# Ten stores at the end of a long convolution and state-space kernel: issued by SyncE instead of GpSimd

## The chip, the cores and the metric

The kernel runs on one core of a Trainium2 chip. The core has five engines, each with its own instruction stream: TensorE (PE in the profile: matmuls; PEld: loading of their stationary operand), VectorE (DVE), ScalarE (ACT), GpSimd (POOL) and SyncE (SP). They meet through semaphores. Data moves between HBM and the on-chip memory by DMA transfers: here SyncE or GpSimd issues them, and 16 DMA engines carry them. The profile counts SyncE's transfers under "hardware_dynamic" (queue q1) and GpSimd's under "software_dynamic" (q0). The metric is the device time of one execution, in microseconds.

## The reference, cut to what matters

Two independent heads work on sequences of 2048 steps and 1024 channels, and their outputs stand side by side in one array of 2048 rows and 2048 columns, in bf16.

```python
# head A: short shift convolution of k, times v; long convolution by FFT; gate with q
kv = k_shift * v
y  = irfft(rfft(pad(kv)) * rfft(pad(ssm_k)))[:S] + kv * ssm_D
a  = q * y
# head B: diagonal complex recurrence
Bu = einsum("bld,pd->blp", x, B_bar)
h[t] = Lam_bar * h[t-1] + Bu[t]
b  = 2 * real(einsum("blp,dp->bld", h, Cmat)) + x * Dskip
out = concatenate([a, b], axis=-1)
```

## The kernel before, in words

Head A turns the long convolution into two levels of small discrete Fourier transforms, done as matmuls against constant tables. Between the levels the data goes through scratch arrays in HBM (`Ys_kv`, `Ys_h`, `Vs`), which is how it is rearranged. The last level is the part that matters here: for each of 16 row groups `n2` SyncE loads a tile from `Vs` (task `vl`, line 694), TensorE multiplies it with a constant (`a3`, line 706) in two halves of 512 columns, ScalarE copies each half out of a PSUM bank (`a3e`, line 713), and for each pair `r` of row groups VectorE multiplies with q in place (`qm`, line 715). The result of a pair, 128 partitions by 2 rows of 1024 columns, 512 KB, is stored by GpSimd into head A's half of the output (`ost`, line 716). There are eight such stores.

Head B goes through the sequence in 16 chunks of 128 steps. For chunk `i`, TensorE projects the input, VectorE rotates, scans and rotates back (`r1` to `r4`, `sc`), TensorE forms the output in two halves of 512 columns, each in four parts (`y`, lines 518 and 521), and ScalarE copies each half out of its PSUM bank into one arena unit (`ye`, line 527). GpSimd stores the whole chunk, 128 rows of 1024 columns, 256 KB, into head B's half of the output (`yst`, line 529). There are sixteen of these.

All tiles lie in one arena of 53 units of 2 KB per partition. The order of the work is written out by hand in one long string, `ORDER`: a word is a task with its arguments and, after a colon, the arena units (a), PSUM banks (p) and other slots that it takes. Tasks are put on their engines in that order, and the framework adds the semaphore waits that the data needs. Each engine carries out its own instructions in order. DMA transfers of SyncE and of GpSimd each use eight semaphores in turn, so a transfer also waits until the one eight before it on the same engine has landed. At the end of the program (line 777) SyncE waits for all transfers, each engine drains, and a handshake led by GpSimd closes the execution.

At the very end, SyncE's last load is `vl.0`. Behind it in `ORDER` come eight stores of head A and the stores of chunks 14 and 15, all on GpSimd:

```python
E["yst"] = lambda i: gpd(out_b[i * T:(i + 1) * T, :], st.pop(("yo", i)))
E["ysp"] = lambda i: spd(out_b[i * T:(i + 1) * T, :], st.pop(("yo", i)))
E["ost"] = lambda r: gpd(oar[:, 2 * r:2 * r + 2, :], st["ot", r])
E["osp"] = lambda r: spd(oar[:, 2 * r:2 * r + 2, :], st["ot", r])
```

Here `gpd` is a transfer issued by GpSimd and `spd` one issued by SyncE; `ysp` and `osp` are there in the kernel before, but `ORDER` doesn't use them.

Of the kernel before, what the change touches and what calls it, by code (L numbers as in the profile page):

```python
# [158 lines left out]
y.14.0.0:p0 y.14.0.1 r2.15:h0 cy.15 vl.7:a40 a3.7.0:p7 y.14.0.2 a3e.15.1 qm.5 ye.13.0 vl.5:a42 y.14.0.3 a3e.12.1 ye.14.0:a34 a3.5.0:p3 vl.13:a28  # L159
a3.13.1:p4 a3.7.1:p5 a3.13.0:p2 a3e.13.0 yst.11 vl.3:a30 a3.3.0:p1 a3.3.1:p6 a3.5.1:p0 a3e.3.0 a3e.7.0:a2 a3e.5.0 vl.6:a10 a3.6.0:p2 a3.6.1:p1 a3e.6.0  # L160
y.14.1.0:p7 a3e.6.1 vl.1:a8 a3e.3.1 y.14.1.1 sc.15.1 vl.9:a16 y.14.1.2 a3e.7.1 a3.9.1:p3 y.14.1.3 yst.13 a3.1.1:p2 a3.9.0:p1 a3.1.0:p6 sc.15.0 a3e.9.1
a3e.5.1 qm.7 vl.0:a48 a3.0.1:p5 a3.0.0:p3 a3e.0.1:a36 r3.15:a12 a3e.9.0 ost.7 r4.15 a3e.0.0 y.15.0.0:p0 y.15.0.1 y.15.0.2 y.15.1.0:p5 y.15.0.3
y.15.1.1 y.15.1.2 ost.5 qm.1 ost.1 qm.3 ye.14.1 ost.3 a3e.1.1 qm.2 a3e.1.0 ost.2 qm.4 qm.0 yst.14 ost.4 a3e.13.1 qm.6 ye.15.0:a52 ost.0 ost.6 y.15.1.3
ye.15.1 yst.15
"""


def full_kernel(ctx, tc, A_q, A_k, A_v, A_shift_k, A_ssm_k, A_ssm_D, B_x, B_Lre, B_Lim, B_Bre, B_Bim,
# [7 lines left out]
    T = 128  # L176
# [6 lines left out]
    out_b = out[0][:, D:2 * D]  # L183
    spd = nc.sync.dma_start
# [45 lines left out]
    st = {}  # L230
# [12 lines left out]
    E = {}  # L243
# [283 lines left out]
        return nc.scalar.copy(st["yo", i][:, dh * 512:(dh + 1) * 512], st.pop(("py", i, dh)))  # L527
    E["ye"] = ye
    E["yst"] = lambda i: gpd(out_b[i * T:(i + 1) * T, :], st.pop(("yo", i)))
    E["ysp"] = lambda i: spd(out_b[i * T:(i + 1) * T, :], st.pop(("yo", i)))  # L530

    def kp(r):
# [180 lines left out]
        return nc.scalar.copy(st["ot", r][:, n2 % 2, dh * 512:(dh + 1) * 512], st.pop(("po", n2, dh)))  # L713
    E["a3e"] = a3e
    E["qm"] = lambda r: nc.vector.tensor_mul(st["ot", r], st["ot", r], st["qt", r])
    E["ost"] = lambda r: gpd(oar[:, 2 * r:2 * r + 2, :], st["ot", r])
    E["osp"] = lambda r: spd(oar[:, 2 * r:2 * r + 2, :], st["ot", r])

# [10 lines left out]
@with_exitstack  # L729
def kernel(  # L730
    ctx: ExitStack,
    tc: tile.TileContext,
    A_q: bass.AP,
    A_k: bass.AP,
    A_v: bass.AP,
    A_shift_k: bass.AP,
    A_ssm_k: bass.AP,
    A_ssm_D: bass.AP,
    B_x: bass.AP,
    B_Lambda_re: bass.AP,  # L740
    B_Lambda_im: bass.AP,
    B_B_re: bass.AP,
    B_B_im: bass.AP,
    B_C_re: bass.AP,
    B_C_im: bass.AP,
    B_log_dt: bass.AP,
    B_Dskip: bass.AP,
    out: bass.AP,
):
    full_kernel(ctx, tc, A_q, A_k, A_v, A_shift_k, A_ssm_k, A_ssm_D, B_x, B_Lambda_re, B_Lambda_im,  # L750
                B_B_re, B_B_im, B_C_re, B_C_im, B_log_dt, B_Dskip, out)
# [30 lines left out]
```

## Time and profile before

| | |
|---|---|
| time, median of 3 runs | 359.53 us (358.28 to 361.29) |
| the profiled execution, its own time | 357.83 us |
| its span, first to last instruction | 356.1 us |
| granted TensorE clock, mean | 0.995 |
| TensorE busy | 333.2 us (94%) |
| VectorE, ScalarE, GpSimd busy | 314.1, 285.4, 87.5 us |
| moved by DMA | 104.10 MB, mean 292 GB/s |

Times of instructions are given in microseconds from the start of the span. A line of the timeline has start, duration, engine, source line, operation, tiles written and read, and in brackets how long the engine had been idle before and for whom it waited. A line with shapes and three numbers joined by slashes gives durations in ns as minimum, median and maximum, and then the first and last start. A stretch shows its length, then for PE, PEld, DVE, ACT and POOL the busy time and the number of instructions, and at the end the granted clock, the busy share of the DMA engines and GB/s. An engine name with a q (SPq, POOLq) is that engine's instruction queue: semaphore and DMA instructions that are not counted as busy.

### The profile page before, as it was taken

How to read it: one execution, taken by the hardware profiler on the slowest of the kernel's cores; microseconds unless marked ns; L12 is line 12 of the kernel's file. 1: busy time of each engine (PE TensorE's matmuls, PEld its weight loads, DVE VectorE, ACT ScalarE, POOL GpSimd, SP SyncE). 2: the span in 40 equal slices, each digit the busy share in tenths (PEclk: the TensorE clock that was granted, in tenths of full speed). 3: DMA queues.
4: the chain of work that ended last, by engine and by line, in shares of the span. 5: the costliest groups of instructions: out<-in, count | busy, mean ns of one | idle time of the engine just before them, and what ended most of it. 6: DMA issues, size and time to landing. Idle time of an engine off the chain costs nothing.

```text
span 356.1 us, 10361 instructions
## 1 busy us (share of the span) xinstructions
PE 333.2 (94%) x4378; PEld 232.8 (65%) x4393; DVE 314.1 (88%) x239; ACT 285.4 (80%) x547; POOL 87.5 (25%) x142
## 2 busy tenths in 40 slices
PE   5999999999999999999979999898989998999991
PEld 2889998465947669766835667464766875944440
DVE  4899999999999999999987997987498769997970
ACT  5899998257799989999578998888989996546550
POOL 5000000021515333436140205121421422300250
PEclk9999999999999999999999999999999999999997
DMA  6999987598999999999989999989889998899973
GB/s 212 319 262 299 234 135 202 195 298 190 297 224 353 317 326 296 276 299 322 323 278 337 327 328 352 307 298 324 312 321 308 349 345 290 330 317 389 371 284 148
DMA packets 62826, 104.10 MB, mean 292 GB/s; under 512 B 29582, under 2 KB 31646, under 8 KB 62780
## 3 DMA queue, kind: packets, MB, share of 16 engines
q1 hardware_dynamic: 50012, 59.78, 59.0%
q0 software_dynamic: 12768, 43.67, 33.6%
q8 instruction: 34, 0.56, 0.7%
q14 instruction: 12, 0.10, 0.1%
HBM read 53.62 MB, written 35.13 MB: 249 GB/s over the span
## 4 chain that ended last, share of the span: by engine, by line
PE 63%; DMA 13%; ACT 10%; issue 6%; DVE 4%; POOL 2%; SPq 1%; POOLq 0%; DVEq 0%; ACTq 0%
PE bank L444 24%; PE bank L518 13%; PE bank L499 6%; DMA wslot<-a_c_W 4%; DMA arena<-arena 4%; PE bank L573 4%; PE bank L611 4%; DMA arena<-Xs 3%; ACT BT L414 3%; PE bank L678 2%; PE bank L595 2%; PE bank L640 2%; DVE gslot L472 2%; PE bank L398 2%; DMA arena<-in_B_B_re_dram 2%
## 5 line engine op out<-in xcount | busy, mean ns | idle before, releaser
L444 PEld LDWEIGHTS <-BT 128*128 128x128 bf16 x2048 | 117.9, 98 | 11.2 <-issue 4.3
L444 PE MATMUL bank<-arena,BT 128*128 128x128 bf16 x2048 | 123.8, 220 | 1.5 <-ACT BT L414 0.8
L472 DVE TENSOR_TENSOR_SCAN gslot<-rtab,gslot 128x1040 bf16<-128x1040 f32 x32 | 72.7, 2310 | 3.9 <-ACT gslot L468 3.5
L518 PE MATMUL bank<-CT,gslot 128*128 128x512 bf16 x275 | 68.7, 379 | 0.7
L499 PE MATMUL bank<-CT,gslot 64*64 64x512 bf16 x896 | 56.3, 376 | 0.4 <-DVE gslot L478 0.4
L666 DVE TENSOR_TENSOR arena<-arena 128x4096 bf16<-128x4096 bf16 x16 | 36.6, 2290 | 17.4 <-ACT arena L656 7.6
L446 ACT CAST arena<-bank 128x512 bf16<-128x512 f32 x64 | 39.0, 641 | 10.1 <-PE bank L444 9.8
L518 PEld LDWEIGHTS <-gslot 128*128 128x128 bf16 x288 | 26.3, 98 | 27.4
L499 PEld LDWEIGHTS <-gslot 64*64 64x64 bf16 x896 | 28.6, 107 | 20.6 <-DVE gslot L478 0.9
L656 ACT CAST arena<-bank 128x512 bf16<-128x512 f32 x64 | 36.2, 658 | 5.6 <-PE bank L640 4.7
L649 ACT CAST arena<-bank 128x512 bf16<-128x512 f32 x64 | 35.0, 637 | 4.7 <-issue 1.5
L617 ACT CAST arena<-bank 128x512 bf16<-128x512 f32 x64 | 35.2, 672 | 4.1 <-PE bank L611 2.9
L686 ACT CAST arena<-bank 128x512 bf16<-128x512 f32 x64 | 35.5, 660 | 3.2 <-PE bank L678 3.0
L579 ACT CAST arena<-bank 128x512 bf16<-128x512 f32 x64 | 35.7, 629 | 2.9 <-PE bank L573 2.9
L459 DVE TENSOR_TENSOR arena<-gslot,Z 128x4096 bf16<-128x4096 bf16 x16 | 36.6, 2289 | 0.7
L459 DVE TENSOR_TENSOR arena<-arena,Z 128x4096 bf16<-128x4096 bf16 x16 | 36.5, 2282 | 0.7 <-ACT arena L446 0.6
L660 POOL DMA_DIRECT2D arena<-arena x32 | 17.4, 547 | 70.6 <-ACT arena L649 60.9
L620 POOL DMA_DIRECT2D Ys_h<-arena x32 | 23.3, 730 | 35.8 <-ACT arena L617 35.8
L640 PE MATMUL bank<-arena,wslot 64*64 64x512 bf16 x256 | 23.7, 382 | 6.8 <-DMA wslot<-a_c_W 4.1
L553 DVE TENSOR_TENSOR arena<-arena 128x4096 bf16<-128x4096 bf16 (+3 forms) x16 | 30.0, 1880 | 0.0
L527 ACT CAST arena<-bank 128x512 bf16<-128x512 f32 x32 | 19.8, 645 | 11.4 <-PE bank L521 9.9
L582 POOL DMA_DIRECT2D Ys_kv<-arena x16 | 11.1, 695 | 64.1 <-ACT arena L579 64.0
(101 smaller groups left out, 421.1 us busy)
## 6 DMA issues: line engine op xcount, KB each, us to landing
Ys_kv<-arena POOLq DMA_DIRECT2D x16, 512.0 KB, 6.5
Ys_h<-arena POOLq DMA_DIRECT2D x32, 256.0 KB, 4.7
arena<-Ys_h SPq DMA_DIRECT2D x16, 512.0 KB, 5.4
arena<-arena POOLq DMA_DIRECT2D x32, 256.0 KB, 4.6
arena<-Ys_kv SPq DMA_DIRECT2D x16, 512.0 KB, 7.7
Vs<-arena POOLq DMA_DIRECT2D x16, 512.0 KB, 6.5
arena<-Vs SPq DMA_DIRECT2D x16, 512.0 KB, 6.7
arena<-in_A_k_dram SPq DMA_DIRECT2D x8, 512.0 KB, 5.4
```

The lines of the kernel that those rows point to most:

```text
L444: nc.tensor.matmul(pu[:, w, jl, :], BT[:, 2 * jp + jl, w, d, :], xT[:, d, :], start=(d == 0), stop=(d == ND - 1))
L446: E["ue"] = lambda i, jp: nc.scalar.copy(st["u", i][:, :, 2 * jp:2 * jp + 2, :], st.pop(("pu", i, jp)))
L459: nc.vector.tensor_mul(m, s_, win(Z))
L472: nc.vector.tensor_tensor_scan(gf, rtab[:].rearrange("p j t -> p (j t)"), gf, 0.0, ALU.mult, ALU.add)
L499: mm = nc.tensor.matmul(st["py", i, dh][64 * c:64 * c + 64, :], h[rows, w, j, 2 + 64 * c:66 + 64 * c], CT[rows, j, w, dh * 512:(dh + 1) * ...
L518: nc.tensor.matmul(py, h[:, w, j, 2:GW], CT[:, j, w, dh * 512:(dh + 1) * 512], start=(j == 0 and w == 0), stop=False)
L579: return nc.scalar.copy(st["ysb", n2][:, p, dh * 512:(dh + 1) * 512], st.pop(("pa", n2, p, dh)))
L617: return nc.scalar.copy(st["yh", hf, s][:, p, e, :], st.pop(("pb", hf, s, e, p)))
L649: return nc.scalar.copy(st["hab", i][:, 0, a, l, :], st.pop(("ps", "h", g, l)))
L656: return nc.scalar.copy(st["x16", i][:, a, l, :], st.pop(("ps", "k", g, l)))
L666: nc.vector.tensor_mul(hab, st.pop(("x16", i)).rearrange("p a l d -> p (a l d)").unsqueeze(1).to_broadcast([P, 2, 2 * D]), hab)
L686: return nc.scalar.copy(st["vsb", i][:, a, dh * 512:(dh + 1) * 512], st.pop(("pv", g, dh)))
```

## The change

The ten stores behind SyncE's last load are issued by SyncE. Eight `ost` become `osp`, `yst.14` becomes `ysp.14`, and the store of the last chunk, `yst.15`, becomes two stores of 512 columns each, by a new task `yh`: the first half stands ahead of the last part of the matmuls of that chunk, the second half at the end. The order of all other tasks and the arena units are as before. GpSimd's last instruction before the end of the program is then `yst.13`.

```diff
@@ -159,9 +159,9 @@
-a3e.5.1 qm.7 vl.0:a48 a3.0.1:p5 a3.0.0:p3 a3e.0.1:a36 r3.15:a12 a3e.9.0 ost.7 r4.15 a3e.0.0 y.15.0.0:p0 y.15.0.1 y.15.0.2 y.15.1.0:p5 y.15.0.3
-y.15.1.1 y.15.1.2 ost.5 qm.1 ost.1 qm.3 ye.14.1 ost.3 a3e.1.1 qm.2 a3e.1.0 ost.2 qm.4 qm.0 yst.14 ost.4 a3e.13.1 qm.6 ye.15.0:a52 ost.0 ost.6 y.15.1.3
-ye.15.1 yst.15
+a3e.5.1 qm.7 vl.0:a48 a3.0.1:p5 a3.0.0:p3 a3e.0.1:a36 r3.15:a12 a3e.9.0 osp.7 r4.15 a3e.0.0 y.15.0.0:p0 y.15.0.1 y.15.0.2 y.15.1.0:p5 y.15.0.3
+y.15.1.1 y.15.1.2 osp.5 qm.1 osp.1 qm.3 ye.14.1 osp.3 a3e.1.1 qm.2 a3e.1.0 osp.2 qm.4 qm.0 ysp.14 osp.4 a3e.13.1 qm.6 ye.15.0:a52 osp.0 osp.6 yh.15.0
+y.15.1.3 ye.15.1 yh.15.1
@@ -527,6 +527,7 @@
     E["yst"] = lambda i: gpd(out_b[i * T:(i + 1) * T, :], st.pop(("yo", i)))
+    E["yh"] = lambda i, dh: spd(out_b[i * T:(i + 1) * T, dh * 512:(dh + 1) * 512], st["yo", i][:, dh * 512:(dh + 1) * 512])
     E["ysp"] = lambda i: spd(out_b[i * T:(i + 1) * T, :], st.pop(("yo", i)))
```

## The prediction

> **What bounds the kernel now.** I read the head of the page first, then the stretches at the end, then what each engine does behind its last useful instruction.
>
> ```profile
> span 356.1 us, 10361 instructions
> ...
> PE 333.2 (94%) x4378; PEld 232.8 (65%) x4393; DVE 314.1 (88%) x239; ACT 285.4 (80%) x547; POOL 87.5 (25%) x142
> ```
>
> ```profile
> 342.00:346.00 4.00, 3.95 (x23) 1.99 (x23) 3.26 (x3) 2.45 (x6) 1.90 (x4) 1.00 0.95 352
> 346.00:350.00 4.00, 2.64 (x15) 1.12 (x13) 0.32 (x1) 1.14 (x2) 1.37 (x3) 1.00 0.94 354
> ```
>
> TensorE bounds everything up to its own last matmul: it is busy for 3.95 of 4.00 us between 342 and 346, and for 2.64 us after 346, which is until 348.64. The column before the last says that the DMA engines are 94 to 95% busy there, with stores alone. No store stands before a matmul, so until 348.64 the stores are covered. What they decide is the 7.4 us between 348.64 and the end at 356.05. In order of time those begin so:
>
> ```profile
> 337.59 3.49 DVE L715 TENSOR_TENSOR arena<-arena 128x2048 bf16<-128x2048 bf16 x3
> ...
> 343.96 2.36 DVE L715 TENSOR_TENSOR arena<-arena 128x2048 bf16<-128x2048 bf16 x2 [0.74 <-ACT arena L713]
> ...
> 345.97 0.58 ACT L527 CAST arena<-bank 128x512 bf16<-128x512 f32 x1 [1.55 <-issue]
> ...
> 346.62 0.72 POOL L716 DMA_DIRECT2D out_dram<-arena  x1 [0.41 <-DVE arena L715]
> ...
> 348.42 0.22 PE L521 MATMUL bank<-Dd,arena 128*128 128x128 bf16 x1
> ...
> 348.68 0.58 ACT L527 CAST arena<-bank 128x512 bf16<-128x512 f32 x1 [2.13 <-PE bank L521]
> 349.56 0.57 POOL L529 DMA_DIRECT2D out_dram<-arena  x1 [2.22 <-ACT arena L527]
> ```
>
> The last matmul ends at 348.64, the last eviction at 349.26, and GpSimd takes up the last store 0.30 us later. The next two answers are for that store alone (from its issue to landing) and for line 777, the end of the program (ns as min/median/max, then first and last start):
>
> ```profile
> L529 POOL DMA_DIRECT2D out_dram<-arena x1: 570/570/570, 349.6 to 349.6; - x1
> ...
> DMA to landing us min/median/max: 2.3/2.3/2.3
> ```
>
> ```profile
> L777 SPq EVENT_SEMAPHORE  x6: 27/28/2082, 349.5 to 349.8; - x6
> ```
>
> ```profile
> L777 SPq DRAIN  x2: 7/10/13, 352.1 to 352.2; - x2
> L777 POOLq DRAIN  x1: 5730/5730/5730, 349.5 to 349.5; - x1
> ```
>
> ```profile
> L777 POOLq EVENT_SEMAPHORE  x4: 17/17/17, 355.3 to 355.9; - x4
> L777 POOLq DRAIN  x3: 51/99/5730, 349.5 to 355.8; - x3
> ```
>
> Here is the point of the whole case. The last store has landed at 349.56 + 2.3 = 351.9. SyncE, which collects all DMAs, sees it (the last of six checks, begun at 349.8, takes 2.08 us, until 351.9) and has drained at 352.2. Then nothing happens for three microseconds, until GpSimd's own drain ends: 349.54 + 5.73 = 355.27. Only then GpSimd takes the others' signals (355.3) and the closing handshake runs, 356.05 - 355.27 = 0.8 us. The wait view says the same from SyncE's side: 3.3 us at line 777. It names TensorE as the releaser, though TensorE had long been done, and the row above it is SyncE's wait for the stores:
>
> ```profile
> SPq L777 <- DMA out_dram<-arena: 23.4, 2, 21.3
> SPq L777 <- PEq L777: 3.7, 2, 3.3
> ```
>
> So the end now has two arms that close in order: the store at 352.2, GpSimd's drain at 355.27. GpSimd's other two drains took 51 and 99 ns with nothing issued since the one before; the long one stands right behind a store.
>
> **The change part by part.** *GpSimd.* Ten stores leave it: eight of 512 KB and two of 256 KB. Its last instruction is then the store of B tile 13, with these rows (issue in ns and its start, then to landing):
>
> ```profile
> L529 POOL DMA_DIRECT2D out_dram<-arena x1: 540/540/540, 329.8 to 329.8; - x1
> ...
> DMA to landing us min/median/max: 6.3/6.3/6.3
> ```
>
> It lands at 336.0. Before, the drain ended 355.27 - 351.9 = 3.4 us after the landing and 355.27 - 350.13 = 5.1 us behind the issue. By either measure it ends between 335 and 340 in the changed kernel, hidden under ten microseconds of TensorE. The arm worth 355.27 - 352.2 = 3.1 us is gone, and next late is SyncE's arm.
>
> *SyncE.* It gains eleven issues. The prices are those of its loads, its last load among them; the first row is the product that its first store waits for:
>
> ```profile
> 333.01 1.20 DVE L715 TENSOR_TENSOR arena<-arena 128x2048 bf16<-128x2048 bf16 x1
> ```
>
> ```profile
> L716 POOL DMA_DIRECT2D out_dram<-arena x8: 710/725/732, 334.5 to 346.6; - x8
> ```
>
> ```profile
> L694 SPq DMA_DIRECT2D arena<-Vs x16: 518/542/1318, 310.5 to 327.7; - x16
> ```
>
> ```profile
> L694 SPq DMA_DIRECT2D arena<-Vs x1: 535/535/535, 327.7 to 327.7; - x1
> ...
> DMA to landing us min/median/max: 9.8/9.8/9.8
> ```
>
> ```profile
> L624 SPq DMA_DIRECT2D wslot<-a_c_W x16: 319/332/2376, 36.7 to 282.6; - x16
> ...
> DMA to landing us min/median/max: 2.7/3.8/5.6
> ```
>
> Eight times 0.54 and three times 0.33 us make 5.3 us, against 8 x 0.725 + 2 x 0.57 = 6.9 us on GpSimd. They cost nothing: SyncE has no other work after 328.2, and consecutive products come 1.16 us apart. The stores wait for the same products in the same order as on GpSimd, so behind a waiting store stand stores only. What they are moved past is the loads: the first store waits for the product that ends at 333.01 + 1.20 = 334.2, and it and the next now stand in one queue behind loads that land until 327.7 + 9.8 = 337.5. They land later than now, the loads perhaps earlier, and neither reaches the end, since TensorE is gapless there. The third store comes after 338.75, when that is over.
>
> *The last store.* What has to be priced is the half tile from SyncE after 349.26; the trace has no SyncE store. Three terms have near rows. SyncE's start behind a producer and its first bytes show at an idle place, where VectorE ends at 69.43 and SyncE's issue starts at 69.46:
>
> ```profile
> 68.21 1.22 DVE L466 TENSOR_TENSOR gslot<-arena 128x2048 bf16<-128x2048 bf16 x1
> ```
>
> ```profile
> 69.46 0.80 SPq L586 DMA_DIRECT2D arena<-in_A_ssm_k_dram  x2
> ```
>
> ```profile
> 69.46:70.40 0.94, 0.94 (x8) 0.45 (x6) 0.94 (x2) 0.94 (x2) 0.17 (x1) 1.00 0.00 0
> 70.40:70.70 0.30, 0.30 (x3) 0.10 (x1) 0.30 (x1) 0.03 (x1) 0.30 (x1) 1.00 0.58 123
> 350.12:350.50 0.38, 0.00 (x0) 0.00 (x0) 0.00 (x0) 0.00 (x0) 0.01 (x1) 1.00 0.06 22
> 350.50:351.50 1.00, 0.00 (x0) 0.00 (x0) 0.00 (x0) 0.00 (x0) 0.00 (x0) 1.00 0.69 262
> 351.50:352.00 0.50, 0.00 (x0) 0.00 (x0) 0.00 (x0) 0.00 (x0) 0.00 (x0) 1.00 0.00 0
> ```
>
> SyncE starts 0.03 us after the producer (I take 0.05; GpSimd's 0.30 is the upper end). No byte moves for 0.94 us, as long as behind GpSimd's last issue (349.56 to 350.50). That store's 256 KB take 1.0 us, so 128 KB take 0.5, and landing is 0.4 us behind the last byte. The sum is 349.26 + 0.05 + 0.95 + 0.5 + 0.4 = 351.2. Then SyncE's remaining waits: 352.2 - 351.9 = 0.3 where the last store's semaphore came late in the list, up to 0.6 (ten steps of 0.06, the spacing of its six checks from 349.5 to 349.8) where it comes early; I take 0.5. With the handshake of 0.8 the span is 352.5, **3.6 us less**. Ends of the range: 1.9 us from issue to landing may be 1.7 or the 2.7 of the fastest 160 KB load, and the waits 0.3 to 0.6, which gives a gain of 2.7 to 4.0.
>
> The Trainium skill (DMA: Bandwidth & Descriptors, section Latency and other measured facts) gives first bytes after some 0.6 us for SyncE's path and about 1 us for GpSimd's. The trace has 0.94 for both, so the measurement stands here; by the skill's figure the sum would be an estimated 0.35 us lower.
>
> *The first half and the reorder.* The first half waits for the eviction that ends at 346.55, just after the store that waits for the last product (346.32). It moves 128 KB ahead of the last matmul. This needs the queue empty when the last half comes at 350.26:
>
> ```profile
> DMA packets 1819, 3.50 MB, mean 389 GB/s; under 512 B 108, under 2 KB 108, under 8 KB 1819
> ...
> q1 hardware_dynamic: 1819, 3.50, 105.0%
> ```
>
> ```profile
> DMA packets 935, 3.40 MB, mean 344 GB/s; under 512 B 105, under 2 KB 105, under 8 KB 935
> ...
> q0 software_dynamic: 935, 3.40, 92.3%
> ```
>
> The upper pair is SyncE's loads from 320 to 329, the lower GpSimd's stores from 340.25 to 350.12. From 339.8 on (338.75 + 0.03 + 0.95) SyncE has six stores of 512 KB, one of 256 and a half: 3.54 MB, 10.3 us at 344 GB/s, done at 350.1. So the last half just finds it empty, with more room at the loads' rate.
>
> Against its own time of 357.83 us (1.8 around its span) the forecast is 354.2. The median shown, 359.53, lies 1.7 above that execution, so I predict 359.53 - 3.6 = **355.9**.
>
> **The rivals.** *The drain stays.* If GpSimd's drain ends 3.4 us after the last store of the program, whoever issued it, only the store's own 0.7 us (351.9 to 351.2) is won: 358.8. For it: the view shows no releaser of that drain, and there is only one case. Against it: the drain stands in GpSimd's own program and starts where that ends. The Trainium skill (same page, section Issuing engines are not separate DMA queues) says that another issuing engine saves only the time of initiating, usually small beside the transfer; that rule points to this rival, and the trace, with 3 us lost behind the landing, does not agree with it.
>
> *Slow stores in one queue (slower).* SyncE's packets are half as long: (1819 - 108) for 3.50 MB are 2 KB each, (935 - 105) for 3.40 MB are 4 KB. If short packets store slowly, all 3.67 MB stand ahead of the landing. The gain is gone when data ends 3.6 us later, at 354.35: 3.67 MB in 14.55 us, 252 GB/s. At 200 GB/s data ends at 358.15 and the time is 358.15 + 0.4 + 0.5 + 0.8 - 356.05 = 3.8 over the median: 363.3. For it: no SyncE store is in the trace. Against: its loads of the same packets run at 389 GB/s.
>
> *The halves collide.* If the second eviction (same arena unit) must wait until the first half has landed, near 350.0, it starts 1.3 us late: 357.2.
>
> **How the numbers follow.** Forecast 0.77, drain stays 0.12, slow stores 0.06, halves collide 0.05. A measurement of this kernel can tell about 1%, 3.6 us, from no change, and the forecast sits right on that bound; its terms reach further down (2.7) than up (4.0), so I give it 0.35 beyond the bound and 0.42 within. Both other gains lie within (0.17), slow stores beyond on the other side (0.05) or just within. With the spread of single runs (358.28 to 361.29): faster 0.36, same 0.59, slower 0.05. The range runs from 354.4 to 358.9 and takes in the drain's rival.
>
> **What would show it.** Right: GpSimd's long drain before 341, SyncE's last wait ending near 351.2, all of line 777's handshake done by 352.5, TensorE's end still at 348.64. Wrong: a GpSimd drain at 354 to 355 (first rival), store bytes running on without a gap past 350.3 (second), the last eviction starting near 350 (third), or a TensorE gap after 330, which would mean that the loads were held up.

## The result and the profile after

The changed kernel takes 355.72 us (median of 16 runs, 352.33 to 358.24), the kernel before 358.97 us (median of 16, 357.42 to 362.28). The ratio is 0.9892, with a 95% interval of 0.9860 to 0.9923: 1.1% faster, 0.8 to 1.4%. Executions more than 1.5% above the fastest of their kernel are left out of the ratios here and below; of the changed kernel's sixteen these are two. The forecast was 355.9 us and 3.6 us less.

The profiled execution has a span of 353.8 us, 2.3 less than before. That is not the gain, because its last matmul ends later. First the head of the page and the timeline's last lines of the changed kernel:

```profile
span 353.8 us, 10363 instructions
...
PE 334.0 (94%) x4378; PEld 234.1 (66%) x4393; DVE 313.8 (89%) x239; ACT 285.1 (81%) x547; POOL 80.5 (23%) x132
```

```profile
349.78 0.22 PE L521 MATMUL bank<-Dd,arena 128*128 128x128 bf16 x1
350.03 0.58 ACT L527 CAST arena<-bank 128x512 bf16<-128x512 f32 x1 [2.13 <-PE bank L521]
350.64 0.34 SPq L530 DMA_DIRECT2D out_dram<-arena  x1
```

TensorE ends at 350.00 instead of 348.64. SyncE's last load, which stands ahead of the first changed instruction, already starts late by as much (329.05 instead of 327.70). From the start of that load to the end of TensorE it is 20.94 us in both profiles. So the 1.36 us come from ahead of the change, which holds TensorE up nowhere behind it, and what compares is the **tail**: the time from the end of the last matmul to the end of the span. It was 356.05 - 348.64 = 7.4 us and is 353.79 - 350.00 = **3.8 us**, 3.6 less.

Now the end of the program, line 779 here, and GpSimd's last store (tile 13):

```profile
L779 SPq EVENT_SEMAPHORE  x11: 17/28/28, 351.0 to 353.7; - x11
L779 POOLq EVENT_SEMAPHORE  x4: 17/17/17, 353.0 to 353.7; - x4
L779 POOLq DRAIN  x3: 51/99/8515, 331.1 to 353.5; - x3
L779 SPq DRAIN  x3: 7/7/13, 352.9 to 353.3; - x3
```

```profile
L529 POOL DMA_DIRECT2D out_dram<-arena x1: 540/540/540, 331.1 to 331.1; - x1
...
DMA to landing us min/median/max: 6.3/6.3/6.3
```

GpSimd's long drain is still there, longer even (8.5 us), but it starts at 331.1 and ends at 339.6, ten microseconds ahead of TensorE's end. GpSimd takes the others' signals at 353.0, as soon as SyncE has drained (352.9 to 353.0). SyncE's list of waits, from the view of waits, now has one long wait of 1.4 us for the store, and the wait for the handshake has shrunk from 3.3 to 0.5 us:

```profile
SPq L779 <- DMA out_dram<-arena: 1.4, 1, 1.4
SPq L779 <- PEq L779: 0.7, 2, 0.5
```

The stretches show the last half tile from issue to landing (length, busy times, clock, DMA share, GB/s):

```profile
341.20:350.00 8.80, 8.74 (x46) 4.10 (x45) 4.82 (x5) 4.11 (x8) 0.00 (x0) 1.00 1.00 372
...
351.00:351.45 0.45, 0.00 (x0) 0.00 (x0) 0.00 (x0) 0.00 (x0) 0.00 (x0) 1.00 0.00 0
351.45:352.05 0.60, 0.00 (x0) 0.00 (x0) 0.00 (x0) 0.00 (x0) 0.00 (x0) 1.00 0.65 219
352.05:352.45 0.40, 0.00 (x0) 0.00 (x0) 0.00 (x0) 0.00 (x0) 0.00 (x0) 1.00 0.00 0
```

Until 350 SyncE's stores run at 372 GB/s. The DMA engines are empty from 351.0, the half's bytes run between 351.45 and 352.05, and it lands at 352.44, 1.8 us behind its issue. SyncE then works through its list until 353.0, and 0.77 us of handshake follow.

### The profile page after: what moved, and what is told of

The parts are those of the page before. It is cut to its first block, busy times and chain, and to the rows that moved or that the text cites. A ratio compares the mean times of both kernels' runs of the same rounds, so it can differ in the third digit from the quotient of the medians.

```text
span 353.8 us, 10363 instructions
## 1 busy us (share of the span) xinstructions
PE 334.0 (94%) x4378; PEld 234.1 (66%) x4393; DVE 313.8 (89%) x239; ACT 285.1 (81%) x547; POOL 80.5 (23%) x132
```

## The experiments

The theory was that the gain is GpSimd's drain, which the change moves off the end. The rivals were a drain that follows the last store whoever issues it, and a gain from the stores' queue or from the halves. All distances below are within one profiled execution; the table at the end of this section puts them together.

**The kernel before, once more.** No edit.

> The kernel before, profiled once more. The changed kernel's profile has TensorE's last matmul end at 350.00 us, the one of before at 348.64, though both run the same instructions up to the change. Theory (executions of one kernel differ by this much ahead of the change): TensorE's end somewhere between 347 and 352 us, the tail from there to the end of the span 7.4 us again. Rival (the change itself costs TensorE 1.4 us): TensorE's end within 0.3 us of 348.64.

```profile
351.22 0.22 PE L521 MATMUL bank<-Dd,arena 128*128 128x128 bf16 x1
```

```profile
L777 POOLq DRAIN  x1: 5732/5732/5732, 352.3 to 352.3; - x1
```

TensorE's end lies at 351.44 this time, 2.8 us later than in the first profile of the same kernel. Yet the tail is 7.42 us and the drain 5.73 us, both within 0.01 of the first. From SyncE's last load, at 330.50 here, to TensorE's end it is 20.94 us again. TensorE's end therefore says nothing of the change, and the tail of one kernel agrees to a hundredth in two profiles.

**Only the last store back on GpSimd.**

```diff
-... osp.0 osp.6 yh.15.0
-y.15.1.3 ye.15.1 yh.15.1
+... osp.0 osp.6
+y.15.1.3 ye.15.1 yst.15
```

> Nine of the ten stores on SyncE, the last one whole on GpSimd. Theory (GpSimd's drain behind its last store is what the change took off the end): a drain of 5 to 6 us right behind that store, tail 7.2 to 7.5 us behind the last matmul, time as before (ratio 1.00). Rival (the nine early stores on SyncE, their shorter issue and clearing of the queue, bring the gain): tail 3.8 to 5 us, ratio 0.99 to 0.993.

Line 779 around the last store:

```profile
L779 SPq DRAIN  x2: 7/10/13, 354.7 to 354.8; - x2
...
L779 POOLq DRAIN  x1: 4958/4958/4958, 352.2 to 352.2; - x1
```

SyncE is done at 354.8, GpSimd's drain at 352.20 + 4.96 = 357.15, and the tail is 6.65 us. One store of ten is enough to bring the drain back to the end, so the rival of the queue falls. But the expected 7.2 us were too many: the drain is 0.77 us shorter than behind ten stores. The ratio, 0.9945 (0.9895 to 0.9995), fits with that, but takes in part of the rival's 0.990 to 0.993 as well; it is the tail that decides.

**Only the last store on SyncE**, nine on GpSimd as before.

```diff
-ye.15.1 yst.15
+ye.15.1 ysp.15
```

> The other way round: only the last store on SyncE, whole; the other nine on GpSimd as before. GpSimd's last store is then issued 2.0 us ahead of the end of the last matmul and lands some 2.2 us behind it. SyncE's own arm alone gives a tail of about 4.2 us. Theory in three forms: if the drain ends 5.1 us behind the issue, the tail is 4.6 us; if 2.2 us behind the landing (as in the changed kernel's profile), 5.2; if 3.4 us behind the landing (as in the profile of before), 6.4. Rival (the drain follows the last landing of any store): 7 us.

```profile
L777 POOLq DRAIN  x3: 51/99/6792, 353.4 to 360.7; - x3
L777 SPq DRAIN  x3: 7/7/13, 358.4 to 360.5; - x3
```

The tail is 5.53 us: SyncE has drained at 358.5, GpSimd's drain ends at 353.40 + 6.79 = 360.19. Its last store landed at 357.65, SyncE's at 358.29. A drain that ends 3.4 us after the last landing of all, 358.29, would have made a tail of 7, and did not. Taken alone this run can't exclude a drain that ends 2 us behind SyncE's store; the changed kernel's own profile does, where the drain was over 12.8 us ahead of the last landing. None of the three forms fitted well: the drain ended 2.5 us behind its own store's landing. TensorE's end lies at 355.45 in this profile, so I use only the distances in its tail; the ratio, 0.9856 (0.9782 to 0.9930), is too wide to place it.

**All ten on SyncE, the last one whole.**

```diff
-... osp.0 osp.6 yh.15.0
-y.15.1.3 ye.15.1 yh.15.1
+... osp.0 osp.6
+y.15.1.3 ye.15.1 ysp.15
```

> All ten stores on SyncE, the last one whole. Theory (halving saves the data time of 128 KB, 0.4 us, but its eleventh transfer puts the last store's semaphore at the head of SyncE's final list, which costs 0.45 us more checks behind the landing than the tenth): tail 3.7 to 3.9 us, no different from the changed kernel's 3.8. Rival (halving is worth its data time, the list nothing): tail 4.2 us or more.

```profile
L531 SPq DMA_DIRECT2D out_dram<-arena x1: 345/345/345, 351.5 to 351.5; - x1
DMA to landing us min/median/max: 2.0/2.0/2.0
```

The whole tile lands 2.02 us behind its issue, only 0.23 more than the half. SyncE then needs 0.15 us to the handshake instead of 0.57. The tail is 3.59 us, 0.2 *less* than with halves and below the expected 3.7 to 3.9 (ratio 0.9866, 0.9815 to 0.9918). The halving brought nothing; its eleventh transfer cost more in the list than it saved in data.

**One store back on GpSimd, the first of the ten.**

```diff
-... a3e.9.0 osp.7 r4.15
+... a3e.9.0 ost.7 r4.15
```

> The changed kernel with the first of the ten stores, ready 14 us ahead of the end of the matmuls, back on GpSimd. SyncE then has ten stores, and the last one takes the eighth of its semaphores, whose check stands last in SyncE's final list. Theory (place in the list costs 0.06 us a step): the checks behind the landing shrink from 0.5 to under 0.1 us, tail 3.35 to 3.45 us; GpSimd's drain ends by 343 or so and doesn't show. Rival (a GpSimd store this late still holds the end): tail over 4 us.

```profile
L779 SPq EVENT_SEMAPHORE  x9: 28/28/28, 350.6 to 352.0; - x9
L779 SPq DRAIN  x1: 13/13/13, 352.1 to 352.1; - x1
```

The last half lands at 351.98, and SyncE's list is at its end with it: eight of the nine checks were passed while the store was under way. GpSimd's drain ends at 343.55. The tail is 3.38 us as expected, 0.41 less than the changed kernel's. In time this is 354.83 us and a ratio of 0.9897 (0.9857 to 0.9937); 0.4 us can't be told in the times, so the tail carries it.

**The same, with the last half evicted by two engines.**

```diff
-y.15.1.3 ye.15.1 yh.15.1
+y.15.1.3 yev.15 yh.15.1
+        nc.scalar.copy(st["yo", i][:, 512:768], py[:, 0:256])
+        nc.vector.tensor_copy(st["yo", i][:, 768:1024], py[:, 256:512])
```

> As e6_one_back, and the last half tile is evicted by two engines: ScalarE its left 256 columns, VectorE its right 256. Theory (the tail is a plain chain of eviction, store, checks and handshake): the 0.58 us eviction shrinks by about 0.2 us, tail 3.1 to 3.3 us, time 1.1 to 1.3% under the kernel before. Rival (two readers of one bank take turns, or VectorE starts late): tail 3.4 us or more.

```profile
348.89 0.37 ACT L531 CAST arena<-bank 128x256 bf16<-128x256 f32 x1 [2.13 <-PE bank L521]
349.30 0.42 DVE L532 CAST arena<-bank 128x256 bf16<-128x256 f32 x1 [2.76 <-ACT arena L531]
349.75 0.34 SPq L535 DMA_DIRECT2D out_dram<-arena  x1
```

VectorE waited for ScalarE (2.76 us idle, released by line 531), so the two quarters ran one after the other: 0.83 us instead of 0.58. The wait named is for ScalarE's write into the arena tile, a semaphore of the program; so the run doesn't show what two engines reading one bank at once would do. The tail is 3.60 us, and the rival's time was right. The ratio, 0.9874 (0.9834 to 0.9915), isn't distinguishable from the version without the split.

**What GpSimd's drain waits for.** The first of these runs adds an instruction to the changed kernel that is no transfer:

```diff
+    E["late"] = lambda i: nc.gpsimd.tensor_copy(late_t[:], st["yo", i][:, 960:1024])
-y.15.1.3 ye.15.1 yh.15.1
+y.15.1.3 ye.15.1 yh.15.1 late.15
```

> The changed kernel with one more instruction on GpSimd at the very end: a copy of 128 by 64 elements of the last evicted half into a tile that nobody reads. Theory (GpSimd's long drain belongs to a store that it issued shortly before): the drain behind the copy takes under 0.5 us, and the tail stays at 3.8 us or as long as the copy needs, under 4.2. Rival (any late instruction on GpSimd makes its drain long): a drain of 3 us or more behind the copy, tail 5 to 7 us.

```profile
L532 POOL COPY late_t<-arena x1: 237/237/237, 350.9 to 350.9; 128x64 bf16<-128x64 bf16 x1
```

```profile
L781 SPq DRAIN  x3: 7/7/13, 353.2 to 355.8; - x3
...
L781 POOLq DRAIN  x2: 108/2349/4590, 350.9 to 355.7; - x2
```

Here my theory fell. A copy of 0.24 us, with GpSimd's last store landed 13 us before, is followed by a drain until 350.90 + 4.59 = 355.49. SyncE was done at 353.26; the tail is 6.05 us. The long drain doesn't belong to a store issued shortly before: it stands behind whatever comes last on GpSimd.

The second puts the four stores before the last one back on GpSimd too:

```diff
-... qm.0 ysp.14 osp.4 a3e.13.1 qm.6 ye.15.0:a52 osp.0 osp.6 yh.15.0
-y.15.1.3 ye.15.1 yh.15.1
+... qm.0 yst.14 ost.4 a3e.13.1 qm.6 ye.15.0:a52 ost.0 ost.6
+y.15.1.3 ye.15.1 yst.15
```

> Last store on GpSimd, and the four before it too; the five earlier ones on SyncE. With one late store on GpSimd the drain ended 2.65 us behind the landing, with all ten 3.4. Theory (the drain grows with the stores that GpSimd issued lately): 2.9 to 3.2 us behind the landing. Rival (it depends on something else, such as SyncE's stores in flight): 2.65 or 3.4 again.

```profile
L779 POOLq DRAIN  x3: 51/108/5322, 351.1 to 357.0; - x3
```

The drain ends at 356.43, 2.97 us behind the landing, between the two values known and as the theory expected; the tail is 7.01 us. It grows with the number of stores. Counted from the end of GpSimd's last instruction, copy, one, five and ten late stores give 4.33, 4.40, 4.72 and 5.13 us: 0.08 us a store, on one line with the copy alone.

The third asks whether *every* transfer of GpSimd counts, or only recent ones. It is the late copy again, with the stores of B tiles 0 to 13 on SyncE:

```diff
-yst.0 ... yst.13   (fourteen words, where they stand)
+ysp.0 ... ysp.13
```

> As e5_late_copy, and the stores of B tiles 0 to 13 are issued by SyncE too, so GpSimd issues fourteen transfers fewer in the whole program (the last of its others is then long landed). Only the drain is looked at; SyncE's loads now queue behind waits for B tiles, which may cost the stages before. The drain ended 4.33 us behind the late copy in e5, 4.40 behind the issue of one late store, 4.72 behind the last of five, 5.13 behind the last of ten: 0.08 us a transfer. Theory (every transfer that GpSimd issued in the program adds 0.08): 3.2 us behind the copy. Rival (a fixed 4.3 us, and only recent transfers add): 4.3 again.

```profile
L532 POOL COPY late_t<-arena x1: 232/232/232, 349.9 to 349.9; 128x64 bf16<-128x64 bf16 x1
```

```profile
L781 POOLq DRAIN  x3: 51/102/3447, 349.9 to 353.8; - x3
```

The drain is 3.45 us long and ends 3.19 us behind the copy, against the 3.2 expected from 0.08 a transfer and the 4.3 of a fixed cost. GpSimd's last transfer here was issued at 305.5 and landed at 308.8, forty microseconds earlier. So transfers long landed are paid for at the end.

The last replaces the copy by a memset, of the kind that GpSimd did at the start of the program:

```diff
+        nc.scalar.copy(late_t[:], st["yo", i][:, 960:1024])
+        nc.gpsimd.memset(late_t[:], 0.0)
```

> As e5_late_copy, but the late GpSimd instruction is a memset of the same small tile, of the kind that GpSimd did at the program's start, behind a small ScalarE copy into that tile. Theory (GpSimd's drain at the end takes 4.3 us behind whatever came last): 4.2 to 4.5 us behind the memset, tail 6.2 to 6.6 us. Rival (the copy is special, a first use of its kind): drain under 0.5 us, tail under 4.3.

```profile
L534 POOL MEMSET late_t<- x1: 152/152/152, 352.2 to 352.2; 128x64 bf16 x1
```

```profile
L784 POOLq DRAIN  x3: 51/108/4502, 352.1 to 357.2; - x3
```

It ends at 352.14 + 4.50 = 356.64, again 4.33 us behind the memset, as expected; the tail is 6.24 us. Copy and memset count alike.

All in one table. "Transfers" counts those that GpSimd issues in the whole program; "behind last" is from the end of GpSimd's last instruction to the end of its drain, "behind landing" from its last landing.

| kernel | tail, us | last on GpSimd | transfers | behind last | behind landing |
|---|---|---|---|---|---|
| before (both profiles) | 7.4 | store | 130 | 5.13 | 3.38 |
| last five on GpSimd | 7.01 | store | 125 | 4.72 | 2.97 |
| only last on GpSimd | 6.65 | store | 121 | 4.40 | 2.65 |
| late memset | 6.24 | memset | 120 | 4.33 | 17.9 |
| late copy | 6.05 | copy | 120 | 4.33 | 17.8 |
| late copy, 14 stores moved | 4.91 | copy | 106 | 3.19 | 44.5 |
| only last on SyncE | 5.53 | store | 129 | 6.04 | 2.54 |
| changed | 3.79 | store, tile 13 | 120 | 7.95 | 2.17 |
| ten on SyncE, whole | 3.59 | store, tile 13 | 120 | 7.98 | 2.17 |
| first of ten on GpSimd | 3.38 | store | 121 | 7.43 | 2.21 |
| the same, two evictions | 3.60 | store | 121 | 7.60 | 2.21 |

In the first six rows the drain follows the last instruction at 0.08 us a transfer: (5.13 - 3.19) / 24 = 0.081. In the last five the last store lands 4.2 to 6.4 us after its issue, and the drain ends 2.2 to 2.5 us behind that landing. The line doesn't go through zero: at 0.081 it would reach it at 67 transfers, and no run went there.

The two join simply. Half of the line's length is 2.16 us for 120 transfers, 2.20 for 121 and 2.52 for 129; the drains behind a late landing are 2.17, 2.21 and 2.54. So all twelve profiles agree, within 0.02 us, with a drain that runs for half of its length behind the last instruction, waits there until GpSimd's last transfer has landed, and then runs the other half. In the first six rows the landing comes 1.75 us behind the last instruction, inside the first half, or 13 us and more ahead of it, so no wait shows. The same rule accounts, to 0.02 us, for the 2.54 us of the run with only the last store on SyncE, which none of its three expected forms did. It is read from the table after the fact; no run was made to test it, and what the drain does in each half isn't shown.

Moving a store also takes bytes and packets off GpSimd's queue and adds a transfer to SyncE. The queue's packets, MB and share, before, with the late copy, and with the late copy and 14 stores moved:

```profile
q0 software_dynamic: 12768, 43.67, 33.6%
```

```profile
q0 software_dynamic: 11456, 38.95, 29.3%
```

```profile
q0 software_dynamic: 10336, 35.28, 26.6%
```

The first step takes off 4.72 MB and 1312 packets for 0.80 us, the second only 3.67 MB and 1120 packets for 1.14 us, so neither bytes nor packets set the length; per transfer both steps are 0.08. SyncE's count doesn't either: the changed kernel and "ten on SyncE, whole" differ by one transfer of SyncE alone (169 and 168), and both end 2.17 us behind the landing. With SyncE's 168 and one transfer more on GpSimd it is 2.21.

## Why the prediction was right, step by step

**GpSimd's drain as the later of two arms, 3.1 us.** Right, and it is nearly the whole gain. The drain ended at 339.6, within the forecast 335 to 340, and the handshake starts with SyncE. Neither of the two measures held, though: it ended 7.95 us behind the last instruction instead of 5.1, and 2.17 behind the landing instead of 3.4. That it fell between them was luck, and with ten microseconds to spare nothing hung on it. What the step said of the cause was wrong: I took the drain for something that belongs to the store ahead of it, from one case. The late copy and the memset show that it stands behind any last instruction, and the runs with 106 to 130 transfers show that its length comes from the transfers of the whole program. The change worked because GpSimd's *last instruction* moved 20 us forward, measured from the end of TensorE (from 1.5 us behind it to 18.4 ahead), not because its last store was taken away.

**The rival that the drain stays with the last store of all** is excluded by the changed kernel's drain, over at 339.6 where the last store lands at 352.4. The rule of the Trainium skill beside it (DMA: Bandwidth & Descriptors, section Issuing engines are not separate DMA queues), that another issuing engine saves only the time of initiating, doesn't agree with the 3.6 us here: it leaves out what a late instruction on GpSimd costs at the end of a program.

**The last store, 351.2 - 349.26 = 1.9 us.** Stretches with their edges close to the first and last bytes, of the kernel before and then of the changed one:

```profile
69.46:70.47 1.01, 1.01 (x8) 0.45 (x6) 1.01 (x2) 0.97 (x2) 0.23 (x1) 1.00 0.00 0
...
350.50:350.69 0.19, 0.00 (x0) 0.00 (x0) 0.00 (x0) 0.00 (x0) 0.00 (x0) 1.00 0.00 0
350.69:351.50 0.81, 0.00 (x0) 0.00 (x0) 0.00 (x0) 0.00 (x0) 0.00 (x0) 1.00 0.85 324
```

```profile
351.00:351.47 0.47, 0.00 (x0) 0.00 (x0) 0.00 (x0) 0.00 (x0) 0.00 (x0) 1.00 0.00 0
351.47:352.01 0.54, 0.00 (x0) 0.00 (x0) 0.00 (x0) 0.00 (x0) 0.00 (x0) 1.00 0.72 243
```

Measured from the end of the eviction: start 0.03 (0.05 forecast), first byte 0.83 (0.95), data 0.54 (0.5), landing 0.43 (0.4), together 1.8. The list of checks cost 0.57 (0.5), the handshake 0.77 (0.8). The tail by the prediction's terms was 352.5 - 348.64 = 3.86 and is 3.79; so close a match owes something to small errors of both signs. The 0.94 us that I read as the first byte of both paths was set by the edges of my stretches: SyncE's load takes 1.01 and GpSimd's last store 350.69 - 349.56 = 1.13 us. For stores the two paths do differ, then, 0.83 against 1.13 us. The page DMA: Bandwidth & Descriptors of the Trainium skill (section Latency and other measured facts) has 0.6 us for SyncE's path and about 1 us for GpSimd's. The trace agrees on the order, with 0.3 us between the two and both figures higher.

**SyncE's issues.** I priced a 512 KB store at 0.54 us by the loads; it took 0.37. The price was hidden under SyncE's idle time, so nothing follows from it. The first two, behind the loads, did not land later than on GpSimd, as I had said: they land 10.98 and 12.22 us after the start of the last load, against 11.08 and 12.29 before. The other six:

```profile
L719 SPq DMA_DIRECT2D out_dram<-arena x6: 372/372/403, 340.2 to 347.7; - x6
...
DMA to landing us min/median/max: 2.8/3.1/3.1
```

```profile
DMA packets 1695, 3.28 MB, mean 372 GB/s; under 512 B 96, under 2 KB 96, under 8 KB 1695
```

**The queue and the slow stores.** For three of these six stores the trace has the landing, 2.8 to 3.1 us after the issue; the same three took 4.0 to 4.2 on GpSimd. Stores in 2 KB packets (3.28 MB in 1695 - 96) run at 372 GB/s between 341.2 and 350, faster than GpSimd's 344, so the rival of slow stores is excluded, and the last half found the queue empty with 0.45 us of room.

**The halves.** They didn't collide: ScalarE starts the second eviction 0.03 us behind TensorE. But the 128 KB that I credited to them with 0.5 us are worth 0.23 (1.79 against 2.02), and the list of checks takes 0.42 back. This term was mis-sized; whole or halved, the kernel is as fast.

**Chances.** I gave "within 1%" 0.59 and "over 1% faster" 0.36. The measured 1.1% lies just on the other side of the bound, which its interval (0.8 to 1.4%) spans. That 355.72 us came within 0.2 of the forecast 355.9 is in part luck: the median of the kernel before went from 359.53 us over three runs to 358.97 over sixteen, so the medians differ by 3.25 us, while the tails of the profiles differ by the forecast 3.6.

## What to carry to other kernels

At the end of a program, look at each engine's drain, not only at the last landing: the later arm is what an edit must shorten, and here it ran 3.4 us behind the last landing. Let GpSimd finish early. With 106 to 130 transfers issued by GpSimd, a store, a copy or even a memset as its last instruction near the end was followed by a drain of 3 to 5 us, and the tail was 1.1 to 3.6 us longer than in the changed kernel. So give the last stores to SyncE, and let GpSimd's own last instruction end some ten microseconds ahead; the longest drain here ended 8.0 us behind it. When the gain is in the tail, measure the tail inside the profile; the ends of TensorE of one and the same kernel lay 2.8 us apart here, more than most of what was to be told apart.

## What the runs showed of the hardware that I had not expected

GpSimd's drain at the end grows with the transfers that it has issued in the whole program, 0.081 us each between 106 and 130, even when the last of them landed 41 us before. The six lengths without a late landing lie within 0.02 us of that line. Behind a store that lands late the drain ends half of that length after the landing, 2.17 to 2.54 us in five profiles with 120 to 129 transfers. The place of the last transfer's semaphore in SyncE's final list is worth up to 0.4 us: each check takes 0.06 us, and those ahead of the one that is waited for are free.
